# Late query blocks: P and q turned by VectorE before their trip through DRAM, and four slots of split queries

## The chip, the cores and the metric

The kernel runs on one core of a Trainium2 chip. The metric is the device time of one execution in microseconds (us), lower is better. Five engines work side by side, each through its own list of instructions in order: TensorE (PE in the profile; PEld is its loading of weights), VectorE (DVE), ScalarE (ACT), GpSimd (POOL) and SyncE (SP), which here does nothing but issue DMA transfers. An instruction that waits holds up everything behind it on its engine. SBUF is the on-chip memory of 128 partitions, PSUM holds what TensorE writes, and DRAM is the memory outside.

## What is computed

Attention with a gated memory, for 4 batches and 8 heads of 576 queries with 64 channels, and then a feed-forward layer on its 2304 x 512 output:

```python
scores = scale * np.matmul(q, k.transpose(0, 1, 3, 2))
scores = np.where(causal, -1000000000.0, scores)
a = np.exp(scores - scores.max(-1, keepdims=True))
a /= a.sum(-1, keepdims=True) + 1e-09
local = np.matmul(a, v)
q_p = phi(q)                                  # phi(x) = where(x > 0, x, exp(x) - 1) + 1
mem_out = (q_p @ M_prev) / ((q_p * z_prev).sum(-1) + 1e-06)
attn = g * mem_out + (1 - g) * local          # g = sigmoid(beta), one per head
h = np.maximum(np.maximum(x @ w1, x @ w2), x @ w3)   # x = attn as [tokens, 512]
out = h @ w_out
```

## The kernel before

**Tiling.** Queries are cut into an early half (rows 0 to 319) and a late half (rows 320 to 575). A pair is two heads of one batch in one half: 32 pairs, the 16 early ones first. Four pairs of one batch and half give one block of x, whose feed-forward work (the MoE pieces, on the PSUM tiles `bm`) is spread over the next four pairs. From pair 10 on (`FLIP`) and so in the whole late half, k and q come from DRAM already block-turned, in runs of 32 elements (128 B), and VectorE finishes the turning in 32 x 32 blocks.

**A late pair.** It has two units of 128 queries. For each head and unit:

- `scores` multiplies split queries (`qs`, a high and a low part in fp32r) with keys (`k1`) into the banks `bs`: 448 columns for the first unit, 2 x 288 for the second. VectorE masks and takes the least value (`masked`, into `p`), ScalarE takes the exponential, GpSimd normalises (`normal`). 64 columns of the memory term stand ahead of each unit in the same tile, so a first unit of P is 128 x 512 and a second one 128 x 640 for each head.
- P must be turned before `values` can multiply it with V (5 blocks of 128, two heads side by side, into `bv`). The second unit is turned by TensorE (`transpose_p`, into `bt`, copied to `pt` by ScalarE or VectorE).
- The first unit goes through DRAM. `swap_out` (line 779) writes it to `pd` with two DMAs in runs of 512 B and reads it back to `kq` with four DMAs of 32 partitions each in runs of 128 B. `swap_in` (line 794) turns the 32 x 32 blocks of `kq` on VectorE into `pt`, 128 x 512 for each head.
- q of a late pair is loaded by `load_qk` (line 547) with eight DMAs of 32 KB into the tile `rw`, each head twice (the low parts need the other half of the partitions), VectorE turns 128 x 256 for each head (`transpose_in`, line 804), and `split_q` (line 847) makes `qs` from it, with ScalarE or VectorE for the high part and VectorE or GpSimd for the low part. Three slots of `qs` serve all pairs, two are taken by each pair. A second copy of q (`rq`, not turned) is loaded for `phi`.

**What sets the order.** The functions only record operations in a `Plan`. `Plan.run` (line 333) is a list scheduler with a table of costs, estimated transfer times (`Plan.move`, line 223) and priorities; `SEEDS` (line 63) shakes the priorities a number of times. What it places is the order of each engine's list, SyncE's too, and the choice between two engines where an operation has two forms. Line 432 issues everything, so the engine and the names of the tiles tell the instructions apart, not the line. Up to the first MoE piece the scheduler puts dummy matmuls (line 396, on `bm` and `mask`) where it sees TensorE idle. Each DMA waits in SyncE's list for what it reads or overwrites.

Of the kernel before, what the change touches and what calls it, by code (L numbers as in the profile page):

```python
# [12 lines left out]
F32 = mybir.dt.float32  # L13
# [12 lines left out]
class Half:  # L26
# [33 lines left out]

NEAR = 2

SEEDS = (
    278295, 305439, 80682, 703233, 480040, 697831, 571163, 590513, 983183, 218641,
    429041, 460242, 338319, 945803, 848882, 158944, 676007, 966563, 564471,
)
# [11 lines left out]
class Plan:  # L78
# [31 lines left out]
    @staticmethod  # L110
    def region(ap):

        if ap.space == bass.MemoryType.DRAM:
            last = sum(st * (n - 1) for st, n in ap.ap)
            return 0, 1, ((ap.offset, ap.offset + last + 1),)
        dims = sorted(((abs(st), n) for st, n in ap.ap[1:] if n > 1 and st), reverse=True)
        row = ap.ap[0][0]
        p0, f0 = divmod(ap.offset, row)
        size = 1
# [6 lines left out]
        return p0, p0 + ap.ap[0][1], tuple((r, r + size) for r in runs)  # L126

# [38 lines left out]
    def cost(self, eng, name, kw):  # L166
# [6 lines left out]
        if eng == "pe":  # L173
            if name == "transpose":
                return 2.5 + 0.837 * kw["in_"].shape[0]
            if kw["rhs"].dtype != F32:
                return 13.3 + kw["rhs"].shape[-1] / 2.4
            if self.mode(name, kw)[0] == 64:
                return 106 + 1.67 * kw["rhs"].shape[-1] if out.shape[0] > 64 else 115
            return 1.69 * kw["rhs"].shape[-1]  # L180
        psum = any(
# [41 lines left out]
    def move(*aps):  # L223
# [6 lines left out]
        for ap in aps:  # L230
# [5 lines left out]
            piece = min(piece, run)  # L236
        return size / (180 if piece < 512 else 240)

# [94 lines left out]
    def run(self, prio, real):  # L333
# [124 lines left out]
def attention_memory_moe(ctx, tc, q, k, v, m_prev, z_prev, beta, w1, w2, w3, w_out, out):  # L458
# [42 lines left out]

    kq = tile_([128, 1280], F32, "rk")
    r_k = Ring.of(kq[:, 512 * i : 512 * i + 512] for i in range(2))
    r_kq = Ring.of(kq[:, 320 * i : 320 * i + 320] for i in range(4))
    r_q0 = Ring(cp, 2, [128, 3, 2, D], F32, "rq")
# [17 lines left out]
    r_in = Ring.of(kq_in[:, 320 * i : 320 * i + 320] for i in range(4))  # L523
    turned_in = kq_in[:, :1024]
    dp = ctx.enter_context(tc.tile_pool(name="dp", bufs=1, space=bass.MemoryType.DRAM))
    r_d = Ring(dp, 2, [8, 128, 128], F32, "pd")
    b_s = Ring(ps, 2, [128, 512], F32, "bs")
# [7 lines left out]
    P = Plan(nc)  # L535
    P.kept |= {t[:].tensor.name for t in r_d.tiles}

    r_w = Ring(cp, 3, [128, 1088], U32, "rw")
    r_g = Ring(cp, 2, [128, 512], F32, "g")
    r_pt = Ring(cp, 2, [128, 1152], F32, "pt")  # L540

# [6 lines left out]
    def load_qk(pi):  # L548
# [12 lines left out]
        else:  # L561
# [231 lines left out]

    def swap_in(pi):

        r = raw[pi]
        for e in range(2):
            r["pt", e] = r_pt.next()
            P.dve.transpose(
                out=r["pt", e][:, :1024].rearrange("p (t x) -> p t x", x=256)[:, :, :128],  # L800
                in_=turned_in[:, 512 * e : 512 * e + 512].rearrange("p (t x) -> p t x", x=128),
            )

    def transpose_in(pi, nm):
# [4 lines left out]
        if pi >= FLIP and nm == "k":  # L809
            for e in range(2):  # L810
                r["k1", e] = r_k1.next()
            for c0 in (0, 320)[: hi + 1]:
                c1 = c0 + HALVES[c0 > 0].n
                src = r_kq.next()[:, : c1 - c0]
                P.dve.transpose(out=src, in_=r["k"][:, c0:c1])
                split_k(pi, c0, c1, src)
            return
        if pi >= FLIP:
# [28 lines left out]
    def split_q(pi, e, src):  # L847

        r = raw[pi]
        n = HALVES[pairs[pi][1]].n  # L850
        r["qs", e] = r_q.next()
        qs = qs_all[:, r["qs", e] : r["qs", e] + 640].rearrange("p (a x) -> p a x", a=2)
        P.copy(("act", "dve"), out=qs[:, 0, :n], in_=src)
        P.combine(("dve", "pool"), ALU.subtract, out=qs[:, 1, :n], in0=src, in1=f(qs[:, 0, :n]))

# [9 lines left out]
    def product(pi, e, q0, rows, c0, c1, s, before=0, after=None):  # L865
# [8 lines left out]
        else:  # L874
            x0 = r["qs", e] + q0
            terms = [
                (qs_all[:, x - before : x + rows], r["k1", e][:, c0:c1]) for x in (x0, x0 + 320)
            ]
# [91 lines left out]
    def transpose_p(pi, e, u):  # L970
        b, hi, hp = pairs[pi]
        hf = HALVES[hi]
        r = raw[pi]
        j, q0, rows, ext = u
        if ("pt", e) not in r:
            r["pt", e] = r_pt.next()
        pt = r["pt", e]
        i = hf.units.index(u)
        p = r["pbuf", e][:, i * hf.pitch : i * hf.pitch + D + ext]
        step = 4 if j < 4 else 3  # L980
# [14 lines left out]
    def values(pi):  # L995
# [5 lines left out]
        for i in range(hf.kb):  # L1001
            c0 = next(u[1] for u in hf.units if u[0] >= i) if i else 0

            xs = [r["pt", e][:, hf.at(i) + c0 : hf.at(i) + n] for e in range(2)]
            for e in (1, 0):
                if not e:
                    P.tied.append(len(P.ops))
                P.pe.matmul(
                    after=xs[1 - e],
                    out=acc[64 * e : 64 * e + 64, c0:n],  # L1010
                    lhsT=r["v"][:, e, i - 1] if i else per_batch["mv", b][:, 2 * hp + e],
# [107 lines left out]
    for n in range(nheads + 2):  # L1119
        pieces = []  # L1120
        sc = pt = None
        if n < nheads:
            pi, e = heads[n]
            us = HALVES[pairs[pi][1]].units
            if pairs[pi][1]:
                sc = [(2 * us[e][3] * 0.425 + 100, partial(scores, pi, x, us[e])) for x in range(2)]
                if e == 0:
                    sc.append((0, partial(swap_out, pi)))
            elif pi >= FLIP:
# [32 lines left out]
        if n < nheads:  # L1162
# [79 lines left out]
```

## Time and profile before

| | us |
|---|---|
| median of 3 runs (lowest, highest) | 512.95 (511.92, 516.84) |
| the profiled execution | 520.21 |
| its span in the trace | 518.4 |
| TensorE busy | 497.5 |
| VectorE, ScalarE, GpSimd busy | 334.7, 296.6, 284.7 |

The profiled execution is 7.26 us longer than the median, so sums made on the trace are carried to the median with care. TensorE's busy time contains dummy matmuls and matmuls at the lower clock. The early pairs fill the first 225 us or so, the late pairs 225 to 478 us, and what is left is the feed-forward work of the last block.

### The profile page before, as it was taken

To read this page: it belongs to the slowest core of one execution; us is meant where nothing else is said; L and a number is where in the kernel's file an instruction comes from. 1 tells how busy PE (TensorE), PEld (TensorE's weight loads), DVE (VectorE), ACT (ScalarE), POOL (GpSimd) and SP (SyncE) were. 2 spreads that over 40 slices of the span, in tenths; PEclk is the share of its full clock that TensorE was granted. 3 is DMA by queue.
4 is the path that set the end of the run, shared out by engine and by line. 5 is a ranking of instruction groups with operands and counts; after the bars stand their busy time and mean duration, and the time that the engine had idled before them with its cause. 6 is when DMAs were issued, how large, how long until landed. Compare 5 with 4: busy or idle time off the path is not lost.

```text
span 518.4 us, 11066 instructions
## 1 busy us (share of the span) xinstructions
PE 497.5 (96%) x3507; PEld 433.2 (84%) x3507; DVE 334.7 (65%) x1137; ACT 296.6 (57%) x844; POOL 284.7 (55%) x444
## 2 busy tenths in 40 slices
PE   8998999999989999999888999799998999999997
PEld 6765788888988899989887789698887989997996
DVE  3699989976655685567456567677678787552120
ACT  4599888765554685466455456465656655543111
POOL 3578887687442583465455467556656667631000
PEclk9999999999989999999998999899999999999999
DMA  6866966645454553358765677878886736443001
GB/s 125 200 170 185 240 194 207 208 93 108 82 104 89 111 98 66 65 123 150 120 121 94 117 166 148 152 130 146 169 156 142 147 101 123 86 80 62 21 1 42
DMA packets 258522, 64.05 MB, mean 124 GB/s; under 512 B 227616, under 2 KB 255520, under 8 KB 258464
## 3 DMA queue, kind: packets, MB, share of 16 engines
q1 hardware_dynamic: 256832, 62.96, 58.3%
q8 instruction: 28, 0.46, 0.4%
q10 hardware_dynamic: 1632, 0.39, 0.3%
q14 instruction: 30, 0.25, 0.2%
HBM read 50.20 MB, written 13.11 MB: 122 GB/s over the span
## 4 chain that ended last, share of the span: by engine, by line
PE 67%; DVE 10%; DMA 9%; SPq 8%; issue 3%; ACT 2%; POOL 1%; ACTq 0%; DVEq 0%; POOLq 0%
PE bm L432 43%; PE bs L432 8%; SPq L432 8%; PE bv L432 7%; PE bt L432 7%; DMA kq<-pd 6%; DVE pt L432 3%; DVE p L432 2%; PE bm L396 2%; DMA rq<-in_q_dram 1%; DMA pd<-p 1%; POOL p L432 1%; DVE sum L432 1%; DVE k L432 1%; DVE bm L432 1%
## 5 line engine op out<-in xcount | busy, mean ns | idle before, releaser
L432 PE MATMUL bm<-xh,wh 128*128 128x320 f32 (+1 forms) x576 | 177.6, 309 | 0.6 <-ACT g L432 0.4
L432 PE MATMUL bm<-xl,wh 128*128 128x320 f32 (+1 forms) x576 | 172.5, 300 | 0.0
L432 PE MATMUL bm<-xh,wl 128*128 128x320 f32 (+1 forms) x576 | 172.0, 299 | 0.0
L432 POOL TENSOR_SCALAR p<-p,sum,gb 128x320 f32<-128x320 f32 (+3 forms) x128 | 86.8, 684 | 53.5 <-DVE sum L432 35.6
L432 PEld LDWEIGHTS bm<-xh,wh 128*128 128x128 f32 x576 | 110.7, 192 | 5.5 <-issue 2.7
L432 PEld LDWEIGHTS bm<-xl,wh 128*128 128x128 f32 x576 | 110.5, 192 | 1.0 <-issue 0.4
L432 PEld LDWEIGHTS bm<-xh,wl 128*128 128x128 f32 x576 | 110.3, 192 | 0.6 <-issue 0.4
L432 ACT ACTIVATE p<-p,st 128x192 f32<-128x192 f32 (+4 forms) x144 | 84.2, 586 | 35.2 <-DVE st L432 33.2
L432 DVE TENSOR_TENSOR t<-bm,t 128x320 f32<-128x320 f32 (+1 forms) x96 | 43.1, 449 | 68.6 <-PE bm L432 67.0
L432 DVE CUSTOM_DVE_ANT_0 p<-bs,mask 128x192 f32<-128x192 f32 (+3 forms) x128 | 59.5, 470 | 26.7 <-PE bs L432 26.4
L432 PE MATMUL bt<-ident,p 128*128 128x128 f32 x336 | 55.3, 278 | 9.4 <-ACT pt L432 5.7
L432 PE MATMUL bs<-k,qs 128*128 128x288 f32 (+5 forms) x264 | 56.8, 320 | 4.3 <-DVE st L432 4.3
L432 ACT COPY pt<-bt 128x256 f32<-128x256 f32 (+2 forms) x134 | 48.4, 388 | 19.9 <-PE bt L432 18.8
L432 PEld LDWEIGHTS bt<-ident,p 128*128 128x128 f32 x336 | 39.8, 140 | 19.2 <-POOL p L432 9.6
L432 POOL TENSOR_TENSOR p<-phf,nn 128x128 f32<-128x128 f32 (+1 forms) x96 | 36.9, 389 | 29.5 <-PE bt L432 15.6
L432 PEld LDWEIGHTS bs<-k,qs 128*128 128x128 f32 (+1 forms) x264 | 40.2, 190 | 7.4 <-DVE st L432 5.8
L432 POOL TENSOR_TENSOR qs<-rk,qs 128x256 fp32r<-128x256 f32 (+1 forms) x35 | 26.9, 770 | 31.6 <-ACT qs L432 25.5
L432 ACT CAST hh<-t 128x256 fp32r<-128x256 f32 x47 | 19.1, 406 | 43.0 <-DVE t L432 42.9
L432 PEld LDWEIGHTS bv<-pt,rv 128*64 128x64 f32 x384 | 28.4, 137 | 15.0
L432 PE MATMUL bv<-pt,rv 128*64 128x256 f32 (+1 forms) x384 | 40.7, 344 | 0.0
L432 DVE STREAM_TRANSPOSE rk<-rw 128x256 f32<-128x256 f32 (+1 forms) x82 | 36.8, 460 | 4.6 <-DMA rw<-in_k_dram 1.7
L432 PE MATMUL bm<-woh,hh 128*128 128x512 f32 (+1 forms) x102 | 39.4, 386 | 0.0
(93 smaller groups left out, 854.0 us busy)
## 6 DMA issues: line engine op xcount, KB each, us to landing
rw<-in_moe_w_dram SPq DMA_DIRECT2D x18, 512.0 KB, 4.1
pd<-p SPq DMA_DIRECT2D x32, 256.0 KB, 2.5
kq<-pd SPq DMA_DIRECT2D x64, 128.0 KB, 3.8
rq<-in_q_dram SPq DMA_DIRECT2D x74, 64.0 KB, 2.4
rw<-in_k_dram SPq DMA_DIRECT2D x64, 72.0 KB, 2.6
rw<-in_q_dram SPq DMA_DIRECT2D x128, 32.0 KB, 2.1
rv<-in_v_dram SPq DMA_DIRECT2D x32, 128.0 KB, 3.1
out_dram<-g SPq DMA_DIRECT2D x15, 256.0 KB, 2.1
```

The source lines that it names most:

```text
L396: self.nc.tensor.matmul(**filler)
L432: getattr(getattr(self.nc, self.ENGINES[e]), name)(**kw)
```

## The change

The P trip: VectorE turns the first unit of P in 32 x 32 blocks before the trip (`turn_p`, in place of `swap_out`), one DMA writes 128 rows of 4 KB to `dp`, and four DMAs read runs of 1 KB straight into `pt` (`move_p`, in place of `swap_in`). `pt` of the late half is one tile whose blocks lie 32 columns apart from each other's, so `values` reads the moving operand in runs of 32 elements, and ScalarE's copies into it write such runs. The second unit's five blocks are copied as 4 + 1 instead of 3 + 2.

The q trip: late pairs no longer load q turned. `turn_q` turns `rq` on VectorE (one 128 x 256 instruction for both heads), writes 128 rows of 1 KB to `dq`, and four DMAs read runs of 512 B into `rw`, from where `split_q` takes it with no further turning.

The split queries of late pairs have four slots of 512 columns instead of three of 640. Only pair 0 (before: pairs 0 and 1) loads its q through ScalarE's queue. The planner counts 110 bytes per ns for runs under 256 B (before: 180) and lets ScalarE begin at 700 ns; there are 26 other `SEEDS` (before: 19).

```diff
-NEAR = 2
+NEAR = 1
-        return size / (180 if piece < 512 else 240)
+        return size / (110 if piece < 256 else 180 if piece < 512 else 240)
-        free["sp"] = 700.0
+        free["sp"] = free["act"] = 700.0
...
-    qs_all = tile_([128, 64 + 3 * 640], F32R, "qs")
-    r_q = Ring.of(64 + 640 * i for i in range(3))
+    qs_all = tile_([128, 2048], F32R, "qs")
+    r_q = [Ring.of(64 + 640 * i for i in range(3)), Ring.of(512 * i for i in range(4))]
...
+    pt_late = pt_all[:, :2048].rearrange("p (a e i r) -> p e i a r", a=8, e=2, i=4)
...
-            for e in range(2):
+            if hi:
+                r["qt"] = t[:, kn : kn + 512]
+            for e in range(2 - 2 * hi):
                 r["qt", e] = t[:, kn + hf.n * e :][:, : hf.n]
...
-    def swap_out(pi):
+    def turn_p(pi):
         r = raw[pi]
-        r["pd"] = d = r_d.next()
         for e in range(2):
-            P.sp.dma_start(
-                out=d[4 * e : 4 * e + 4].rearrange("t q x -> q t x"),
-                in_=r["pbuf", e][:, :512].rearrange("q (t x) -> q t x", t=4),
+            P.dve.transpose(
+                out=turned_p.rearrange("p (c e i r) -> p e i c r", c=4, e=2, i=4)[:, e],
+                in_=r["pbuf", e][:, :512].rearrange("p (i c x) -> p i c x", i=4, c=4),
             )
+        r["pd"] = d = r_dp.next()
+        P.sp.dma_start(out=d, in_=turned_p)
+
+    def move_p(pi):
+        src = raw[pi]["pd"].rearrange("(a x) m -> x a m", x=32)
         for c in range(4):
             P.sp.dma_start(
-                out=turned_in[32 * c : 32 * c + 32].rearrange("r (k x) -> r k x", x=32),
-                in_=d[:].rearrange("k (a r) x -> r (k a) x", r=32)[:, :, 32 * c : 32 * c + 32],
+                out=pt_all[32 * c : 32 * c + 32, :1024].rearrange("p (a m) -> p a m", a=4),
+                in_=src[:, :, 256 * c : 256 * c + 256],
             )
-    def swap_in(pi):
-        r = raw[pi]
-        for e in range(2):
-            r["pt", e] = r_pt.next()
-            P.dve.transpose(
-                out=r["pt", e][:, :1024].rearrange("p (t x) -> p t x", x=256)[:, :, :128],
-                in_=turned_in[:, 512 * e : 512 * e + 512].rearrange("p (t x) -> p t x", x=128),
+    def turn_q(pi):
+        r = raw[pi]
+        t = r_qt.next()
+        P.dve.transpose(
+            out=t.rearrange("p (h b r) -> p b h r", h=2, b=4),
+            in_=r["q"].rearrange("p c e (h x) -> p (c e) h x", h=2),
+        )
+        d = r_dq.next()
+        P.sp.dma_start(out=d, in_=t)
+        src = d.rearrange("(a x) m -> x a m", x=32)
+        for g in range(4):
+            h = g % 2
+            P.sp.dma_start(
+                out=r["qt"][32 * g : 32 * g + 32].rearrange("p (a m) -> p a m", a=4),
+                in_=src[:, :, 128 * h : 128 * h + 128],
             )
...
+                xs = [pt_late[:, e, i] for e in range(2)]
...
-                sc.append((0, partial(swap_out, pi)))
+                sc.append((0, partial(turn_p, pi)))
...
+                if pairs[pi + 1][1]:
+                    tr.append((0, partial(turn_q, pi + 1)))
...
-            pieces.append((0, partial(swap_in, heads[n][0])))
+            pieces.append((0, partial(move_p, heads[n][0])))
```

**VectorE's list, at the first unit of a late pair.** The `ISA p,st` rows are the masks (448 columns for the first unit, 288 for the second), `k_3_85` is a split key, `t` an MoE tile. Before, this stands there:

```order
L432 ISA p,st<-bs_113,mask 128x448
L432 ISA st 128x1
L432 TENSOR_TENSOR k_3_85<-rk,k_3_85 64x256
L432 STREAM_TRANSPOSE pt_128<-kq 128x4x128
L432 STREAM_TRANSPOSE pt_129<-kq 128x4x128
L432 TENSOR_SCALAR sum<-sum 128x1 x2
L432 STREAM_TRANSPOSE rk<-rw_124 128x320
L432 RECIPROCAL sum<-sum 128x1 x2
L432 ISA p,st<-bs_114,mask 128x448
```

Behind the masks of a later late pair the change has:

```order
L436 TENSOR_SCALAR sum<-sum 128x1
L436 TENSOR_TENSOR t_104<-bm_120,t_104 128x256
L436 RECIPROCAL sum<-sum 128x1
L436 STREAM_TRANSPOSE kq<-p 128x4x4x32 x2
L436 TENSOR_TENSOR t_104<-bm_121,t_104 128x256
L436 ISA p,st<-bs_115,mask 128x288
L436 ISA st 128x1
```

A few rows ahead of these, the change turns q of the next pair (`rq` to `rk`), between the two 288-column masks that precede the pair's first-unit masks:

```order
L436 ISA p,st<-bs_115,mask 128x288
L436 ISA st 128x1
L436 STREAM_TRANSPOSE rk<-rq_90 128x4x2x32
L436 ISA p,st<-bs_116,mask,st 128x288
L436 ISA st 128x1
L436 TENSOR_TENSOR k_1_83<-rk,k_1_83 64x320
L436 ISA p,st<-bs_115,mask 128x448
```

Before, the two turnings of P read `kq`, which a DMA fills, and stand between the two masks of the next pair; now they read `p`, which GpSimd writes, and stand behind both masks of their own pair.

**SyncE's list over about one late pair.** `rw` from `in_q` is q, `rw` from `in_k` is k, `rv` is v, `rq` is q for phi. Before:

```order
L432 DMA rw_124<-in_q_dram 32x8x32
L432 DMA kq<-pd_112 32x32x32 x4
L432 DMA rv_96<-in_v_dram 128x4x64 x2
L432 DMA rw_124<-in_q_dram 32x8x32 x7
L432 DMA z_93<-in_z_prev_dram 128x256
L432 DMA rw_125<-in_q_dram 32x8x32 x4
L432 DMA pd_111<-p 128x4x128
L432 DMA rw_125<-in_k_dram 32x18x32 x2
L432 DMA pd_111<-p 128x4x128
L432 DMA rq_90<-in_q_dram 128x2x64 x2
L432 DMA rw_125<-in_k_dram 32x18x32 x2
```

And in the change:

```order
L436 DMA dp_111<-kq 128x1024
L436 DMA rw_125<-dq_114 32x4x128 x4
L436 DMA rq_90<-in_q_dram 128x2x64 x2
L436 DMA rv_97<-in_v_dram 128x4x64 x2
L436 DMA pt<-dp_111 32x4x256 x4
L436 DMA dq_113<-rk 128x256
L436 DMA rw_125<-in_k_dram 32x18x32
L436 DMA rw_126<-dq_113 32x4x128 x4
L436 DMA dp_112<-kq 128x1024
L436 DMA rq_91<-in_q_dram 128x2x64 x2
```

The eight short loads of q are gone, two writes of P have become one, and one write and four reads of q have come in; both reads stand a few rows behind the write whose landing they wait for.

**ScalarE's list between two pairs' scores.** Before, where the second-unit copies to `pt` end and the next pair's keys are split:

```order
L432 COPY pt_129<-bt_116 128x256
L432 ACTIVATE phf_88<-rq_91 128x256
L432 CAST hh<-t_104 128x256
L432 CAST k_2_84<-rk 64x320
L432 ACTIVATE p,sum<-p,st 128x576
```

And in the change:

```order
L436 COPY pt<-bt_118 128x128
L436 ACTIVATE phf_88<-rq_91 128x256
L436 CAST qs<-rw_126 128x256
L436 CAST hh<-t_104 128x256
L436 CAST k_2_84<-rk 64x320
L436 CAST k_2_84<-rk 64x256
L436 ACTIVATE p,sum<-p,st 128x576
```

The cast that makes split queries now reads `rw`, which the q trip fills, and not `rk`, which VectorE fills.

## Rows read from the trace of the kernel before

**Rows 1.** Page, part 4, and the chain of waits of 225 to 478 us by line

```profile
PE 67%; DVE 10%; DMA 9%; SPq 8%; issue 3%; ACT 2%; POOL 1%; ACTq 0%; DVEq 0%; POOLq 0%
by line: PE bm L432 31.3%; DMA kq<-pd 12.9%; SPq L432 12.4%; PE bv L432 8.9%; PE bs L432 7.2%; DVE pt L432 4.5%; PE bt L432 4.0%; issue 3.8%; DVE p L432 2.8%; DMA pd<-p 2.2%; POOL p L432 1.6%; DVE k L432 1.5%; DVE sum L432 1.1%; DVE rk L432
```

**Rows 2.** Waits of PE, 225 to 478 us: total us, times, longest

```profile
PE bs L432 <- DVE st L432: 4.3, 4, 2.1
PE bt L432 <- POOL p L432: 3.2, 2, 3.0
PE bt L432 <- ACT pt L432: 3.0, 1, 3.0
PE bv L432 <- issue: 0.9, 1, 0.9
```

**Rows 3.** Windows: length, busy PE PEld DVE ACT POOL, PEclk, DMA share, GB/s

```profile
100.00:225.00 125.00, 122.31 (x816) 110.67 (x815) 81.17 (x292) 74.21 (x231) 67.08 (x113) 0.99 0.48 92
225.00:350.00 125.00, 116.60 (x804) 104.21 (x804) 78.09 (x270) 67.98 (x186) 71.68 (x105) 0.97 0.73 136
350.00:478.00 128.00, 124.74 (x931) 110.25 (x928) 84.24 (x287) 70.74 (x194) 73.34 (x103) 1.00 0.64 123
420.00:475.00 55.00, 54.63 (x416) 48.49 (x415) 32.62 (x112) 28.27 (x78) 28.89 (x42) 1.00 0.51 96
```

**Rows 4.** Timeline, PE at three stalls: start, us, work, [idle before <-releaser]

```profile
260.63 0.74 PE L432 MATMUL bt<-ident,p 128*128 128x128 f32 x5 [3.03 <-ACT pt L432]
...
330.36 0.77 PE L432 MATMUL bt<-ident,p 128*128 128x128 f32 x5 [2.96 <-POOL p L432]
...
390.59 0.54 PE L432 MATMUL bs<-k,qs 128*128 128x288 f32 x2 [1.36 <-DVE st L432]
```

**Rows 5.** Timeline, VectorE shortly ahead of those three stalls

```profile
256.79 1.30 DVE L432 STREAM_TRANSPOSE pt<-kq 128x512 f32<-128x512 f32 x2 [4.22 <-DMA kq<-pd]
...
327.37 1.30 DVE L432 STREAM_TRANSPOSE pt<-kq 128x512 f32<-128x512 f32 x2 [3.50 <-DMA kq<-pd]
...
388.60 1.30 DVE L432 STREAM_TRANSPOSE pt<-kq 128x512 f32<-128x512 f32 x2 [2.25 <-DMA kq<-pd]
```

**Rows 6.** Waits of VectorE, 225 to 478 us: total us, times, longest

```profile
DVE pt L432 <- DMA kq<-pd: 25.0, 12, 4.2
```

**Rows 7.** Timeline, SyncE's list around one pair's reading of P

```profile
284.44 2.92 SPq L432 DMA_DIRECT2D rw<-in_q_dram  x6
287.41 2.59 SPq L432 DMA_DIRECT2D kq<-pd  x4
```

**Rows 8.** DMA issues of 300 to 360 us: count, KB each, median us to landing

```profile
pd<-p SPq DMA_DIRECT2D x8, 256.0 KB, 2.4
kq<-pd SPq DMA_DIRECT2D x16, 128.0 KB, 3.8
rw<-in_q_dram SPq DMA_DIRECT2D x36, 32.0 KB, 2.5
rw<-in_k_dram SPq DMA_DIRECT2D x14, 72.0 KB, 2.6
```

**Rows 9.** Landing of all reads of P, from the view of the tile kq

```profile
DMA to landing us min/median/max: 2.6/3.8/5.5
```

**Rows 10.** Groups by shape on VectorE: busy us, mean ns, idle before

```profile
L432 DVE STREAM_TRANSPOSE pt<-kq 128x512 f32<-128x512 f32 x32 | 20.9, 690 | 25.0 <-DMA kq<-pd 25.0
L432 DVE STREAM_TRANSPOSE rk<-rw 128x256 f32<-128x256 f32 x48 | 20.3, 432 | 1.3 <-POOL qs L432 0.9
```

**Rows 11.** Chain of waits in order of time: start, us, what

```profile
12.38 3.00 PE bm L396 x27
...
423.79 2.10 PE bv L432 x20
...
425.89 0.73 PE bs L432 x4
...
430.85 1.43 PE bm L432 x12
...
473.68 0.76 PE bt L432 x5
```

More of the change, by code (lines that the diff above doesn't have):

```diff
@@ L58 @@
 FILL_GAP, FILL_WARM, FILL_FROM, WARM = 60, 80, 450, 7500
[L61 removed]
+NEAR = 1
 SEEDS = (
[L64 to L65 removed]
+    170495, 618851, 839998, 870954, 887498, 687841, 346258, 191154, 388799, 372867,
+    129018, 780087, 981015, 378067, 878635, 152620, 533197, 991412, 299355, 70786,
+    899701, 937121, 576273, 847781, 388742, 446033,
 )
@@ L115, in region @@
             return 0, 1, ((ap.offset, ap.offset + last + 1),)
-        dims = sorted(((abs(st), n) for st, n in ap.ap[1:] if n > 1 and st), reverse=True)
         row = ap.ap[0][0]
+        dims = sorted(
+            ((abs(st), n) for st, n in ap.ap[1:] if n > 1 and st and st % row), reverse=True
+        )
         p0, f0 = divmod(ap.offset, row)
+        p1 = p0 + ap.ap[0][1] + sum(st // row * (n - 1) for st, n in ap.ap[1:] if st % row == 0)
         size = 1
@@ L125, in region @@
             runs = [r + i * st for r in runs for i in range(n)]
-        return p0, p0 + ap.ap[0][1], tuple((r, r + size) for r in runs)
+        return p0, p1, tuple((r, r + size) for r in runs)
     @staticmethod
@@ L176, in cost @@
             if kw["rhs"].dtype != F32:
-                return 13.3 + kw["rhs"].shape[-1] / 2.4
+                return 13.3 + n / 2.4
             if self.mode(name, kw)[0] == 64:
-                return 106 + 1.67 * kw["rhs"].shape[-1] if out.shape[0] > 64 else 115
-            return 1.69 * kw["rhs"].shape[-1]
+                return 106 + 1.67 * n if out.shape[0] > 64 else 115
+            return 1.69 * n
         psum = any(
@@ L813, in transpose_in @@
                 c1 = c0 + HALVES[c0 > 0].n
-                src = r_kq.next()[:, : c1 - c0]
+                src = kq[:, c0:c1] if hi else r_kq.next()
                 P.dve.transpose(out=src, in_=r["k"][:, c0:c1])
                 split_k(pi, c0, c1, src)
+            return
+        if hi:
+            for e in range(2):
+                split_q(pi, e, r["qt"].rearrange("p (a c e r) -> p e c a r", a=4, c=2, e=2)[:, e])
             return
@@ L849, in split_q @@
         r = raw[pi]
[L850 to L854, printed above, removed]
+        hi = pairs[pi][1]
+        n = HALVES[hi].n
+        r["qs", e] = o = r_q[hi].next()
+        hl = [qs_all[:, x : x + n] for x in (o, o + n)]
+        if hi:
+            hl = [x.rearrange("p (c a r) -> p c a r", c=2, a=4) for x in hl]
+        P.copy(("act", "dve"), out=hl[0], in_=src)
+        P.combine(("dve", "pool"), ALU.subtract, out=hl[1], in0=src, in1=f(hl[0]))
     def split_k(pi, c0, c1, src):
@@ L876, in product @@
             terms = [
-                (qs_all[:, x - before : x + rows], r["k1", e][:, c0:c1]) for x in (x0, x0 + 320)
+                (qs_all[:, x - before : x + rows], r["k1", e][:, c0:c1]) for x in (x0, x0 + HALVES[pairs[pi][1]].n)
             ]
@@ L974, in transpose_p @@
         j, q0, rows, ext = u
+        i = hf.units.index(u)
+        p = r["pbuf", e][:, i * hf.pitch : i * hf.pitch + D + ext]
+        if hi:
+            t = b_t.next()
+            for i in range(4):
+                P.pe.transpose(
+                    out=t[:, 128 * i : 128 * i + 128], in_=p[:, 128 * i : 128 * i + 128], identity=ident
+                )
+            P.copy(
+                ("act", "dve"),
+                out=pt_late[:, e, :, 4:],
+                in_=t.rearrange("p (i a r) -> p i a r", i=4, a=4),
+            )
+            t = b_t.next()[:, :128]
+            P.pe.transpose(out=t, in_=p[:, 512:640], identity=ident)
+            P.copy(("act", "dve"), out=pt_all[:, 2048 + 128 * e : 2176 + 128 * e], in_=t)
+            return
         if ("pt", e) not in r:
@@ L1002, in values @@
             c0 = next(u[1] for u in hf.units if u[0] >= i) if i else 0
-            xs = [r["pt", e][:, hf.at(i) + c0 : hf.at(i) + n] for e in range(2)]
+            if not hi:
+                xs = [r["pt", e][:, hf.at(i) + c0 : hf.at(i) + n] for e in range(2)]
+            elif i < 4:
+                xs = [pt_late[:, e, i] for e in range(2)]
+            else:
+                xs = [pt_all[:, 2048 + 128 * e : 2176 + 128 * e] for e in range(2)]
             for e in (1, 0):
```

21 lines of the change are left out of this document (12 added, 9 removed).

## The prediction

> **What bounds the kernel now.** I read the page first: the chain that ended last is TensorE for two thirds of the span, and next to it stand DMA and SyncE's list with 9% and 8% [rows 1]. So TensorE is the bound, and time can only be had where it waits. In the stretch of the late pairs the same chain looks otherwise: the reading back of P (`kq<-pd`) holds 12.9% of it and SyncE's own issuing 12.4% [rows 1]. TensorE's waits there add up to 4.3 + 3.2 + 3.0 + 0.9 = 11.4 us in 8 waits [rows 2], and the windows say the same: 253 us less 116.60 and 124.74 busy leave 11.7 [rows 3]. The granted clock is 0.97 in the first of these windows and 1.00 in the second [rows 3]. A mean of 0.97 over 125 us is time at 1.2 GHz instead of 2.4; it has cost 0.03 x 125 = 3.7 us of work. Loss in the late pairs: 11.4 + 3.7 = 15.1 us of the profiled 520.21.
>
> Who causes the waits? TensorE names three different engines [rows 2], so I looked at what VectorE did just before the longer ones. Each time it had stood still for the reading of P: TensorE idle 3.03, 2.96 and 1.36 us [rows 4], VectorE idle before turning `kq` 4.22, 3.50 and 2.25 us [rows 5]. The reader is to see one cause under three names: VectorE's list is in order, the turning waits for the DMA, and the masks behind it hold up ScalarE, GpSimd and in the end TensorE. All in all VectorE waited 25.0 us in 12 such waits [rows 6]. The differences 1.19, 0.54 and 0.89 us, 0.9 in the mean, are what the other engines absorb: a wait of an engine off the bound costs about its length less 0.9 us.
>
> Why the reading is late is in SyncE's list: six loads of q, 2.92 us, directly ahead of the four readings, which take 2.59 to issue [rows 7], and these land 3.8 us after issue in the median, 5.5 at worst [rows 9].
>
> **The change, part by part.**
>
> *P trip.* On VectorE nothing is saved in count: two 128 x 512 turnings of 0.690 us [rows 10] a pair, before and after. What changes is what they wait for: GpSimd's result and not a DMA. That takes all 25.0 us of VectorE's waits on `kq<-pd` away, and with them the stalls of [rows 4]. The new place has a cover: the turned rows go to DRAM, come back and are read by TensorE in `values`, which stands about a pair later; nothing else waits for them. The length of this trip, from the last turning on: the write lands in 2.4 us by the pd row of half its size, or 3.8 as an upper bound; then four issues (2.59) and 3.8 to land [rows 7, 8], 8.8 to 10.2 us together. A late pair takes about 14 us, and the turnings stand behind the first unit's masks, so `values` finds them landed, with some 4 us to spare. The reads now overwrite `pt` and must wait for the preceding `values` (2.10 us [rows 11]); that ends before the write has landed, so I cost it at nothing. If that cover were gone, SyncE would stand still, and loads of k and v behind it would come late.
>
> *Packets.* By sizes and run lengths, a late pair moves P and q in 1024 + 4096 + 2048 = 7168 packets before, and in 128 + 512 + 128 + 512 = 1280 after; k's 2304 of 128 B stay. DMA was busy 0.73 and 0.64 in these windows [rows 3]. I cost this at no time of its own: it only makes landings shorter, between nothing and the 1.2 us by which the median 3.8 stands over the minimum 2.6 [rows 9]. The Trainium skill (DMA: Bandwidth & Descriptors, Specifications) asks for at least 512 B for full rate, which P's reads and q's now reach; the trace agrees in kind, as 128 KB in 128 B runs took 3.8 us and 256 KB in 512 B runs 2.4 [rows 8].
>
> *SyncE.* A pair issued 2 + 4 for P and 8 for q; now 1 + 4 and 1 + 4. Four issues of 0.49 us (2.92 / 6 [rows 7]) are saved, 2 us a pair. Against it stands one more wait for a landing, dq's, with at most one or a few rows of cover in the list: up to 2.4 us [rows 8]. I count the two as even.
>
> *q trip.* VectorE does one 128 x 256 turning instead of two, 0.432 us less a pair [rows 10], off the bound. But q now arrives over two landings, and ScalarE's cast waits for the second. From the order: the turning stands between the 288-column masks; the cast stands behind the copies of the second five transposes. Between lie 36 matmuls at 1.43 us for 12, ten transposes at 0.76 for five, and the four 448-column score matmuls, 0.73 x 448 / 288 = 1.1 us [rows 11]: 6.9 us, less about 0.9 for mask and turning, 6.0 us. The trip takes 2.4 for the write, three further issues of 0.49, and 2.5 to 3.8 for the last read [rows 7, 8], 6.4 to 7.7 us. So ScalarE waits 0.4 to 1.7 us a pair. With 0.9 us absorbed, the lower end costs nothing and the upper 0.8 us a pair, 12.8 us over 16 pairs. I take the lower half, because DMA has fewer packets in flight, and cost it at nothing, and keep the rest for a rival.
>
> The Trainium skill (DMA: Bandwidth & Descriptors, Anatomy of one DMA) speaks against such trips: some 2 us of each transfer are completion, most of all for writes to DRAM, whatever their size. The shortest median here, 2.4 us [rows 8], agrees; by the rule the q trip would be 4.0 us plus issues and bytes, which changes no term above.
>
> *Four slots.* The second head's cast need no longer wait for the preceding pair's scores. It was one cause of slack, not of a stall among [rows 2]; a gain of 0.
>
> *Strided operand of values.* TensorE reads four of five blocks in runs of 32 elements. No row before shows such an operand. Below: nothing. Above: a matmul of 256 columns takes 1.43 / 12 = 0.119 us [rows 11], 0.012 more than 256 columns at 2.4 GHz; if each further run cost as much, 7 x 0.012 for each of eight pairs of strided matmuls are 0.7 us a pair of heads, 11 us in all, an estimate from that row. I take 0, since within a run it reads as before. The Trainium skill (SBUF — State Buffer, Door 1: The DMA port swizzle, its note on cachelines) would have only the 16-byte step matter, and a run here is eight of them; no run shows it yet.
>
> *Start.* By the order, 135 dummies stand before the first `values` instead of 116. At 3.00 us for 27 [rows 11] that is 0 to 2.1 us; I take 1.0.
>
> *What stays.* A new plan has stalls of its own. The quietest stretch, 420 to 475, lost 0.4 us in 55; the stretch ahead of the late pairs, without P trips, 2.7 idle and 0.01 x 125 = 1.3 by the clock in 125 [rows 3]. Over 253 us that is 1.7 to 8.1 us; middle 4.9.
>
> **The sum.** 15.1 - 4.9 - 1.0 = 9.2 us off the profiled 520.21, that is 511.0. The median is 7.26 lower. If that excess has nothing to do with these stalls, the median becomes 512.95 - 9.2 = 503.7. If all of it is these stalls, the median has only 7.8 of 15.1 to lose: (15.1 - 4.9) x 7.8 / 15.1 - 1.0 = 4.3, or 508.7. I take the middle, **506.2**.
>
> **Rivals.**
> 1. *Same: the waits only change their engine.* ScalarE (q cast) waits at the middle of its range and somewhat over, 1.3 us: 0.4 x 16 = 6.4 us back, and the median comes to 506.2 + 6.4 = 512.6. For it: the trip has no slack by the sum above. Against it: 25.0 us of VectorE's waits are gone, and ScalarE is less busy than VectorE [rows 3].
> 2. *Slower: the q trip bounds the pair.* If the last read lands 5.5 us after issue, as the worst of kq did [rows 9], the trip is 9.4 us, ScalarE waits 3.4, TensorE 2.5 a pair: 40 us, and even half of the pairs give 506.2 + 20 = 526. It decides from a wait of about 1.9 us a pair on: (1.9 - 0.9) x 16 = 16 us against the 9.2 gained. Against it: those 5.5 us were among 7168 more small packets.
> 3. *Strided operand.* At its bound of 11 us: 517, still no change. Nothing in the rows speaks for it.
> 4. *All stalls go*: 512.95 - 15.1 + 1.0 = 498.9. The quiet stretch [rows 3] speaks for it, the start and the chance that the median had fewer stalls against it.
>
> **How the numbers follow.** Forecast with its own spread (500 to 510) 0.62, all stalls gone 0.06, rivals 1 and 3 0.20, rival 2 0.12. About 1% is what a measurement here can tell from no change: 507.8 and 518.1. Of the forecast's 0.62, 0.52 lie below 507.8. Faster 0.52 + 0.06 = 0.58; same 0.10 + 0.20 = 0.30; slower 0.12. The range reaches from 499 to 515, which leaves out rival 2, the far end of rival 3 and a little below; the likeliest case's own range is 500 to 510.
>
> **What would show it.** Right: no wait of VectorE on a DMA of P, the turnings behind GpSimd; VectorE's 25.0 us gone; TensorE's waits in the late pairs under 6 us; DMA share well under 0.7 there; granted clock 1.00 in all late windows. Wrong: ScalarE or GpSimd waiting on `rw<-dq` for more than 1 us in most pairs; TensorE waiting on `pt<-dp` at `values`; `values` longer than 2.10 us for 20 matmuls; SyncE standing still ahead of `pt<-dp` with k late behind it; the first `values` more than 2 us later.

## The result, and the profile after

| | before | after |
|---|---|---|
| median (lowest, highest), us | 514.89 (511.92, 517.37), 4 runs | 500.74 (500.31, 501.68), 4 runs |
| profiled execution, us | 520.21 | 501.68 |
| its span, us | 518.4 | 499.6 |

The ratio of after to before is 0.973, with a 95% interval of 0.9665 to 0.9795: faster by 2.7%. (A fourth run of before, 517.37, moved its median from 512.95.) One execution of `before_newplan` below took 514.12 us at a mean granted clock of 0.977, where its other five had 0.993 to 0.997, and is left out of its figures.

The chain that ended last, by engine and by line, of the whole of after:

```profile
PE 88%; ACT 3%; DVE 3%; DMA 2%; SPq 2%; issue 1%; POOL 0%; ACTq 0%; DVEq 0%
PE bm L436 57%; PE bv L436 11%; PE bs L436 10%; PE bt L436 9%; SPq L436 2%; DMA rq<-in_q_dram 1%; PE bm L400 1%; DMA rw<-in_moe_w_dram 1%; DVE k L436 1%; ACT p L436 1%; DVE p L436 1%; ACT pt L436 0%; ACT kq L436 0%; POOL p L436 0%; ACT phe L436 0%
```

TensorE holds 88% of it where it held 67% [rows 1]; no transfer of P is in it any more. All waits of TensorE in the late pairs (which now end at about 465 us), as total, times, longest:

```profile
PE bt L436 <- POOL p L436: 0.6, 2, 0.3
```

Before, these were 11.4 us [rows 2]. The windows of the late pairs (length, busy PE, PEld, DVE, ACT, POOL, granted clock, DMA share, GB/s) have TensorE busy for all but 0.7 of 240 us, at a clock of 1.00 in both, where it was 0.97 in the first [rows 3]:

```profile
225.00:350.00 125.00, 124.68 (x875) 111.28 (x875) 91.91 (x305) 73.52 (x203) 71.09 (x102) 1.00 0.62 159
350.00:465.00 115.00, 114.58 (x877) 102.25 (x874) 74.21 (x252) 62.92 (x171) 57.07 (x82) 1.00 0.45 126
```

Of VectorE's waits in the same stretch, these two rows answer to the 25.0 us of [rows 6]. The turnings wait a little for GpSimd, as the code says, and the turning of q for its load:

```profile
DVE kq L436 <- POOL p L436: 4.2, 11, 0.7
...
DVE rk L436 <- DMA rq<-in_q_dram: 1.7, 2, 1.3
```

The new transfers (count, KB each, median us from issue to landing):

```profile
dp<-kq SPq DMA_DIRECT2D x16, 512.0 KB, 3.1
pt<-dp SPq DMA_DIRECT2D x64, 128.0 KB, 3.1
...
rw<-dq SPq DMA_DIRECT2D x64, 64.0 KB, 2.1
```

**Where the time went.** From the first `values` of the last early pair to that of the last late pair before took 475.53 - 229.81 = 245.7 us and after 456.69 - 226.15 = 230.5. These 15.2 us are the 15.1 that the prediction had called the loss of the late pairs, all of it. Another 3.7 (229.81 - 226.15) lie in the early pairs, nearly all of them behind the start: the fourth pair's `values` begins at 46.32 us in before and at 46.05 in after. From there to the last early pair before took 183.5 us and after 180.1; runs with before's very lists for the early pairs took 180.5 to 183.1 (`q_merged`, `swap_deferred`, `kq_long` below), so up to 3 us of it is how before's profiled execution fell out.

### The profile page after: what moved, and what is told of

Read it like the earlier page. It is cut to its first block, busy times and chain, and to the rows that moved or that the text cites. A ratio compares the mean times of both kernels' runs of the same rounds, so it can differ in the third digit from the quotient of the medians.

```text
span 499.6 us, 10997 instructions
## 1 busy us (share of the span) xinstructions
PE 489.8 (98%) x3528; PEld 426.9 (85%) x3528; DVE 342.3 (69%) x1152; ACT 292.6 (59%) x832; POOL 274.0 (55%) x425
## 4 chain that ended last, share of the span: by engine, by line
PE 88%; ACT 3%; DVE 3%; DMA 2%; SPq 2%; issue 1%; POOL 0%; ACTq 0%; DVEq 0%
PE bm L436 57%; PE bv L436 11%; PE bs L436 10%; PE bt L436 9%; SPq L436 2%; DMA rq<-in_q_dram 1%; PE bm L400 1%; DMA rw<-in_moe_w_dram 1%; DVE k L436 1%; ACT p L436 1%; DVE p L436 1%; ACT pt L436 0%; ACT kq L436 0%; POOL p L436 0%; ACT phe L436 0%
## 5 line engine op out<-in xcount | busy, mean ns | idle before, releaser
L436 PEld LDWEIGHTS bm<-xh,wh 128*128 128x128 f32 x576 | 109.5, 190 | 5.1 <-issue 1.9
L436 PEld LDWEIGHTS bm<-xh,wl 128*128 128x128 f32 x576 | 108.9, 189 | 0.3
L436 ACT ACTIVATE p<-p,st 128x320 f32<-128x320 f32 (+4 forms) x144 | 84.1, 585 | 22.5 <-DVE st L436 20.3
L436 ACT COPY pt<-bt 128x256 f32<-128x256 f32 (+4 forms) x135 | 49.6, 388 | 29.3 <-PE bt L436 28.4
L436 PE MATMUL bt<-ident,p 128*128 128x128 f32 x336 | 56.7, 280 | 4.2 <-ACT pt L436 3.4
L436 PE MATMUL bs<-k,qs 128*128 128x288 f32 (+5 forms) x264 | 54.9, 312 | 0.0
L436 PE MATMUL bv<-pt,rv 128*64 128x256 f32 (+1 forms) x384 | 42.4, 345 | 0.0
L436 PE MATMUL bm<-woh,hl 128*128 128x512 f32 (+1 forms) x102 | 39.0, 383 | 0.3 <-DVE hl L436 0.3
L436 PE MATMUL bm<-wol,hh 128*128 128x512 f32 (+1 forms) x102 | 38.6, 381 | 0.0
```

The costliest lines, as they stand in the source:

```text
L436: getattr(getattr(self.nc, self.ENGINES[e]), name)(**kw)
```

## Experiments

Three theories went into them. A: VectorE's wait, and what stands behind it in its list. B: P simply comes back late, because of short packets and SyncE's list. C: the planner's new constants and seeds. The runs were made in three groups, each beside its own runs of before: 512.81 us for the first (`p_alone`, `q_alone`, `after_oldplan`, `wait_back`), 514.24 for the second (those of 3 and 4) and 514.68 for the third (those of 6 and `before_newplan`). Gains are against the group's own before.

**1. Each trip alone.** `p_alone` is the change without its q trip, its four slots and its planner's numbers:

```diff
-    r_q = [Ring.of(64 + 640 * i for i in range(3)), Ring.of(512 * i for i in range(4))]
+    r_q = Ring.of(64 + 640 * i for i in range(3))
...
-                if pairs[pi + 1][1]:
-                    tr.append((0, partial(turn_q, pi + 1)))
```

> The P trip alone: VectorE turns P first, runs of 4 KB out and 1 KB in, straight into the operand of values; q, the three slots, the planner's constants and the seeds are those of before. Theory A (VectorE standing still for the reading of P is what stalls TensorE): about 502 us, -12, and no wait of VectorE on a DMA of P. Theory B (late landings: short packets and SyncE's long list; q's eight short loads are still there): 506 to 510. Theory C (the new seeds and constants bring the gain): 514, give or take 5, since its seeds were not found for it.

Measured: 498.93 us (497.26 to 500.09), ratio 0.9716 (0.9669 to 0.9764). TensorE has no wait at all left in its late pairs, and VectorE none for a DMA. The P trip alone does all that the change does, and more than any of the theories had expected of it.

`q_alone` is the other half: q trip and four slots, with `swap_out` and `swap_in` as before and the old planner's numbers.

> The q trip and the four slots alone, P as before, planner and seeds of before. Theory A: 511 to 515, and VectorE still waits some 20 us on the reading of P. Theory B: 504 to 508, since SyncE has four issues and 2048 packets less a pair and P's reads come earlier. Theory C: 514 give or take 5.

Measured: 503.39 us (502.82 to 504.83), ratio 0.981 (0.9764 to 0.9856). It leaves P's trip as it was, and yet two thirds of the gain are there. VectorE's waits for transfers in the late pairs:

```profile
DVE rk L435 <- DMA rq<-in_q_dram: 9.8, 7, 3.2
DVE pt L435 <- DMA kq<-pd: 8.0, 10, 2.6
```

The wait for P fell from 25.0 to 8.0 us although P's readings landed no sooner (median 3.9 us): VectorE comes to the turning 3.2 us behind their last issue in the median, where it came after 2.2 in before. 13.9 and 9.4 us don't add up to the 12 to 14 of both: the two halves remove the same stalls.

**2. The planner's numbers, taken back and put in alone.** `after_oldplan` is the change with before's `NEAR`, rate, start and seeds.

> The changed kernel with the seeds, the constants and the start of before. Theories A and B: 501 to 504, a microsecond or two over the changed kernel for want of fitting seeds. Theory C: 510 or more.

Measured: 499.47 us (498.73 to 501.96), ratio 0.9746 (0.9689 to 0.9802). The change needs none of them, and I put theory C aside. That was too quick. The opposite run, `before_newplan`, is the kernel before with those numbers only:

```diff
-        return size / (180 if piece < 512 else 240)
+        return size / (110 if piece < 256 else 180 if piece < 512 else 240)
```

> The kernel before with the change's planner alone: 110 bytes per ns for short runs, ScalarE from 700 ns on, one pair's first loads instead of two through ScalarE, and the 26 new seeds; every operation and transfer as before. Theory C (the new plan is the gain): 500 to 504 us. Theory B (P comes back late): short runs are now counted as slower by the planner, so it may leave the reading back more room; I expect half of the stalls at most to go, 507 to 513 us, and VectorE to wait 12 us or more for the reading back of P.

Measured: 506.12 us (505.41 to 507.36), ratio 0.9845 (0.9816 to 0.9874): 8.6 us, with every operation and transfer of before. VectorE, for which I had expected 12 us or more, waits for P no more at all; the one wait for a transfer in its late pairs is

```profile
DVE rk L433 <- DMA out_dram<-g: 1.6, 1, 1.6
```

P lands as late as ever (min/median/max, from the view of the tile `kq`), and the DMA share from 225 to 350 us is higher than before, not lower, while TensorE doesn't stand still there for a moment (its 3.7 us of waits in the late pairs come behind 350 us):

```profile
DMA to landing us min/median/max: 2.7/3.8/5.1
```

```profile
225.00:350.00 125.00, 125.00 (x880) 112.09 (x879) 84.29 (x294) 75.88 (x208) 81.64 (x116) 1.00 0.79 150
```

What differs is where the turning stands. One pair, SyncE's list and then VectorE's:

```profile
297.16 2.46 SPq L433 DMA_DIRECT2D kq<-pd  x4
```

```profile
305.33 1.30 DVE L433 STREAM_TRANSPOSE pt<-kq 128x512 f32<-128x512 f32 x2
```

From the end of the last issue (299.62) to the turning are 5.7 us, and there is no wait in brackets. In before the issues of [rows 7] end at 290.00, and the turning that reads them is this one:

```profile
293.60 1.30 DVE L432 STREAM_TRANSPOSE pt<-kq 128x512 f32<-128x512 f32 x2 [3.95 <-DMA kq<-pd]
```

VectorE was there at 289.65, before the last issue had ended. Over all 16 late pairs VectorE comes to the turning 0.7 us before to 4.1 us after the last issue in the kernel before (median 2.2), and 5.1 to 9.9 us after it here (median 6.4). The 3.8 us of a landing are counted from each issue's own start; from the end of the last issue, P has landed after 2.7 to 3.9 us in before (median 3.4) and after 3.0 to 4.6 here (median 3.3). By the planner's old rate four readings of 131072 B take 4 x 131072 / 180 = 2.9 us, by the new one 4.8. I did not part the rate from the 26 seeds, `NEAR` and ScalarE's start.

**3. Only the place of VectorE's turnings.** `swap_deferred` is before with these two instructions let go ten rows later in VectorE's list (or ahead of the first that needs them), all other lists untouched:

```diff
+            op.hold = 10
...
+                if op.hold:
+                    held.append(op)
```

> The kernel before, with one edit: VectorE's two turnings of P (kq to pt) stand ten instructions later in its list; every other list, all transfers and the plan are those of before. Theory A (masks queued behind the wait are what stalls TensorE): VectorE's 25 us of waits on P's reading shrink to a few us and the time falls by 6 to 12 us, to 501 to 507. Theory B (it is the transfers' own lateness that has to go; the data come too late in any case): values is then held up itself, 511 to 515.

Measured: 511.46 us (507.5 to 512.94), ratio 0.9923 (0.9894 to 0.9952), 2.8 us. VectorE's wait is gone (1.5 us of 25.0 are left; it now comes 2.2 to 9.1 us after the last issue), but TensorE waits in a new place (total, times, longest):

```profile
PE bv L440 <- DVE pt L436: 4.6, 3, 2.4
PE bv L440 <- ACT p L440: 1.5, 1, 1.5
PE bv L440 <- ACT k L440: 1.5, 1, 1.5
PE bv L440 <- ACT phe L440: 1.3, 1, 1.3
PE bv L440 <- DVE sum L440: 0.9, 1, 0.9
```

9.8 us at `bv`, the `values`, and 11.3 with the other waits, in place of 11.4 elsewhere: `values` now begins 0.2 us (median) behind the end of the turnings, and P has landed 2.0 us (median) before they begin. A later turning without a later or better placed `values` moves the stall to the reader of `pt`. Theory A, by which it is enough to take VectorE's wait away, does not hold in this form; other distances than ten rows were not tried.

**4. Only the transfers.** Three runs change what is issued, and leave every list as planned. `kq_long` reads P back in runs of 1 KB (512 packets a pair instead of 4096):

```diff
+            op.real = dict(
+                out=turned_in[32 * c : 32 * c + 32].rearrange("p (a m) -> p a m", a=4),
+                in_=rows[:, :, 256 * c : 256 * c + 256],
+            )
```

> The kernel before with P's four reads in runs of 1 KB instead of 128 B (4096 packets a pair become 512), the same bytes, the same lists; P comes back in another arrangement, which changes values and no work. If packets are what makes P's reads late: the reads land in about 3 us instead of 3.8, 503 to 508. If SyncE's list is: 510 to 514, since each read is issued as late as before.

Measured: 502.58 us (501.31 to 504.42), ratio 0.9761 (0.9718 to 0.9803): 11.7 us by run length alone. The landing's median went from 3.8 to 3.3 us, and a read takes less time to issue, too (ns, min/median/max, in before and in `kq_long`):

```profile
L432 SPq DMA_DIRECT2D kq<-pd x64: 320/562/2397, 232.9 to 467.1; - x64
...
L434 SPq DMA_DIRECT2D kq<-pd x64: 320/430/1678, 230.1 to 450.2; - x64
```

From the first issue to the last landing P takes 5.0 us (median) instead of 6.2. VectorE's wait went from 25.0 us to

```profile
DVE pt L434 <- DMA kq<-pd: 10.7, 7, 3.9
```

`q_merged` loads late q in four DMAs of 64 partitions instead of eight, so that SyncE has four issues fewer a pair ahead of P's readings, with the same packets:

```diff
+                        op.real = "none" if i % 2 else dict(
+                            out=to[32 * i : 32 * i + 64].rearrange("p (c d) -> p c d", d=32),
```

> The kernel before with late q loaded in four DMAs of 64 partitions instead of eight of 32, the same bytes in the same runs of 128 B, the plan's lists otherwise untouched; rows of q land on other partitions than they should, which changes values and no work. It takes four issues of about 0.5 us a pair from SyncE's list and leaves every packet. If SyncE's list is what makes P's reads late: 502 to 507 and VectorE's waits under 10 us. If packets are: 511 to 515.

Measured: 509.53 us (505.23 to 511.38), ratio 0.9892 (0.9834 to 0.995), 4.7 us, between what the two theories had expected; P's landing is unchanged (3.9), and VectorE's wait is

```profile
DVE pt L434 <- DMA kq<-pd: 17.2, 13, 4.2
```

So SyncE's list was a cause too, by these medians the smaller one.

`p_short` goes the other way: the full change, with P read in runs of 128 B again.

> The changed kernel with P's four reads in runs of 128 B instead of 1 KB, as before the change, the same bytes, the same lists; P comes back in another arrangement, which changes values and no work. If packets carry the gain: 505 to 510. If who waits carries it (nothing but values waits for these reads now, a few us later): 500 to 502, with landings near 3.8 us.

Measured: 501.46 us (499.68 to 502.44), ratio 0.9743 (0.9704 to 0.9783), no slower than the change by anything that could be told. The transfer itself is slower again:

```profile
pt<-dp SPq DMA_DIRECT2D x64, 128.0 KB, 3.8
```

It took 3.1 in the change, and TensorE's waits in the late pairs are the same 0.6 us. The same 4096 packets a pair that cost 11.7 us in before cost nothing here, with q's short loads gone as well; P turned first, in short runs and with before's loads of q, was not run.

**5. VectorE's wait put back.** `wait_back` is the change with one small copy on VectorE that waits for P's four readings, as `swap_in` did:

```diff
+        P.dve.tensor_copy(out=mask_top[:, :1], in_=pt_all[:, :1])
```

> The changed kernel with one tiny VectorE copy a late pair (one column of pt) that waits for the landing of P's four reads, recorded where swap_in was. Theory A: VectorE waits again, 16 waits of up to 2 us, and the time rises by 3 to 10 us over the changed kernel. Theory B: the landings are early now, the copy finds them done, under 1 us more. Theory C: nothing.

Measured: 500.68 us (499.45 to 501.72), ratio 0.9752 (0.9706 to 0.9798). The copy hardly waited:

```profile
DVE mask_top L436 <- DMA pt<-dp: 1.8, 2, 1.6
```

So this run could not price the wait: the planner put the copy behind the landing in most pairs. It shows that a VectorE instruction that needs this transfer costs nothing that can be measured where it comes after the landing.

**6. The slots, and the change beside the P trip on one chip.** `three_slots` takes the fourth slot away:

```diff
-    r_q = [Ring.of(64 + 640 * i for i in range(3)), Ring.of(512 * i for i in range(4))]
+    r_q = [Ring.of(64 + 640 * i for i in range(3)), Ring.of(512 * i for i in range(3))]
```

> The full change with three slots of split queries in the late half instead of four. My step said that the fourth slot is worth 0: within 1 us of the full change. If the slot is what gives the query trip its time, ScalarE's cast waits for the preceding pair's scores and the time is 505 or more. The planner's lists move a little too, since the slot is one of the things that it waits for; a difference of 1 to 2 us would be put down to that.

Measured: 500.97 us (499.32 to 502.88), ratio 0.9741 (0.9711 to 0.977). The fourth slot is worth nothing that can be measured.

`changed_again` and `p_again` are the change and `p_alone` once more, in the same group.

> The full change once more, on the same chip as the next three, so that differences under one per cent between them can be read. All theories: 500 to 501.5 us, ratio 0.97 to 0.98 to the kernel before.

> The P trip alone (old q loads, three slots, the planner's old constants and seeds), beside the full change on one chip. If late landings of P were all that cost (theory B), nothing is left for the q trip and the slots to remove once the P trip is there: within 1.5 us of the full change, on either side. If the q trip and the slots have a gain of their own, this kernel is 2 us or more slower than the full change; if the q trip costs something by itself (a second landing for each pair), it is 1.5 us or more faster.

Measured: 501.44 us (499.42 to 503.82), ratio 0.9747 (0.9712 to 0.9781), and 499.03 (497.61 to 501.28), ratio 0.9709 (0.9678 to 0.974). The P trip alone is ahead by 2.4 us here, as it was, with 498.93, in the first group; the intervals overlap, so I claim only that the q trip and the slots add nothing to it. Nor are the 2.4 us the price of the q trip, since `p_again` has before's planner too. The pair that differs in the q trip and the slots alone is `after_oldplan` and `p_alone`, in one group: 499.47 and 498.93 us, 0.5 apart, with ranges that overlap. The P trip with before's planner is the fastest kernel of the study.

**All of them on one scale.** For each profiled execution, the length of the stretch from the first `values` of the last early pair to that of the last late pair, TensorE's waits in the late pairs, and the difference (us):

| | stretch | TensorE's waits | difference |
|---|---|---|---|
| before | 245.7 | 11.4 | 234.3 |
| `swap_deferred` | 241.9 | 11.3 | 230.6 |
| `q_merged` | 235.6 | 4.9 | 230.7 |
| `before_newplan` | 234.6 | 3.7 | 230.9 |
| `q_alone` | 233.9 | 2.9 | 231.0 |
| `kq_long` | 233.1 | 3.3 | 229.8 |
| after | 230.5 | 0.6 | 229.9 |
| `p_alone` | 229.4 | 0 | 229.4 |

In before, 3.7 us of the clock come on top [rows 3], which leaves 230.6; in the other seven the granted clock is 1.00 in this stretch. So the late pairs take 229 to 231 us of TensorE's work in every one, and the runs differ in the waits that they leave and in whether the clock falls. That is also why 14.3 us less of VectorE's waits are worth so much in `kq_long`: 8.1 us of TensorE's waits and the 3.7 us of the clock are gone with them. The 0.9 us that the prediction has the other engines absorb in each wait fits roughly: 10.7 - 7 x 0.9 = 4.4 us for `kq_long` (measured 3.3), 17.2 - 13 x 0.9 = 5.5 for `q_merged` (4.9), 25.0 - 12 x 0.9 = 14.2 for before (11.4); for `q_alone`, 8.0 us in 10 waits, it would leave nothing (2.9).

## Why the prediction was right, and where its sum was off

The direction, the range and the core of the mechanism held; the forecast of 506.2 was 5.5 us too high, and the measured 500.74 lies next to rival 4 (498.9), which I had given 0.06. Point by point:

- **One cause under three names: right.** All of VectorE's 25.0 us are gone, and the 15.1 us of the late pairs with them (15.2 between the two `values` above). But the place of the turnings is not the only cure. `swap_deferred` takes VectorE's waits away and keeps TensorE's, and the longer runs of the P trip, which I had priced at nothing, bring 11.7 us without it (`kq_long`). What all the stalls have in common is P coming back too late for the first instruction that needs it; each trip moves that, and so does the new plan alone, and how the gain divides among them cannot be read from these runs.
- **What stays, 4.9 us: the step that failed.** TensorE waits 0.6 us in the late pairs, at a clock of 1.00. I had taken the new plan's stalls from other stretches of before (1.7 to 8.1 us). The runs show what I should have looked at: the room. In before, the turning stood in the middle of P's way, 2.2 us (median) behind the end of the last issue, for a landing 3.4 behind it, while `values` stood 5.0 to 13.8 us behind it (median 8.5). The change takes the turning out of that stretch; what then waits for the landing is `values` alone, and its distance from the last issue is still 5.0 to 13.0 (median 8.6), for a landing 2.8 behind it. The distances in before could be read beforehand, and gave no reason for a remainder. My "some 4 us to spare" for this place was about right (1.9 us at least, 5.8 in the median), and I didn't let it bear on the sum.
- **Start, a loss of 1.0 us: about right in size, in the wrong place.** Where the start ran undisturbed (last section), `values` of the fourth pair begins at 44.8, 44.1 and 44.7 us with the new planner's start (`wait_back`, `p_short`, `three_slots`) and at 43.4, 43.4, 42.9, 43.7, 43.8 and 43.5 with the old one (`p_alone`, `q_alone`, `after_oldplan`, `swap_deferred`, `q_merged`, `kq_long`): 1 us later. But the first `values`, which 19 more dummies were to delay, begins no later, at 19.8 us in those three and at 19.8 to 20.8 in those six. Between the two TensorE waits no longer (1.4 to 2.2 us against 1.6 to 3.0), so what costs the 1 us stays open. And 3.00 us for 27 dummies [rows 11] was not their usual price (last section). The new plan wins the loss back in the early pairs behind the start: `values` of the last early pair begins at 224.2 us (mean of those three) against 225.0 (mean of those six), 0.8 us earlier, which I had not looked for.
- **From the profile to the median: wrong.** I let half of the stalls be a peculiarity of the slow profiled execution. The median lost 14.2 us (12.2 from the first three runs), so the stalls were in the usual runs in full. The profiled execution was long for other reasons, at least in part: its fourth `values` begins 2.5 to 3.4 us later than in the six just named. With 15.1 less 0.6, and 0.8 for the early pairs, the whole 15.3 us taken from 512.95 give 497.7, and from 514.89 give 499.6; measured are 500.74.
- **Packets, at no time of their own: right for the changed kernel, wrong for before.** `p_short` shows nothing for 4096 packets a pair and `kq_long` 11.7 us. The 1.2 us by which P is back sooner decide only where an instruction in order stands at the landing's edge. The rule of the Trainium skill (DMA: Bandwidth & Descriptors, Specifications) that runs should be of 512 B or more agrees in kind: 128 KB landed in 3.8 us in runs of 128 B and in 3.1 in runs of 1 KB, in the same list.
- **SyncE, even: not wholly.** Four issues fewer were worth 4.7 us in before (`q_merged`). In the change SyncE stands still 9.6 us in 4 waits for `dq`'s landing, and TensorE's late waits name no transfer.
- **q trip, 0 of 0.4 to 1.7 us a pair: right.** ScalarE has no wait for `rw<-dq` among those of 225 to 465 us; its casts wait for a free slot, that is for TensorE (total, times, longest):

```profile
ACT qs L436 <- PE bs L436: 19.2, 8, 3.4
```

  So the cast is held by the scores ahead, not by the second landing, and rivals 1 and 2 did not come. The trip's landings are 1.7 to 4.3 us (median 2.2). The Trainium skill's rule on some 2 us of fixed cost, most of it completion (DMA: Bandwidth & Descriptors, Anatomy of one DMA), was measured there on transfers that GpSimd issues, which the prediction does not say. These here, which SyncE issues, agree with it, but it speaks against nothing where the time is covered.
- **Four slots, 0: right** (`three_slots`). But the slack that I had seen in them did not come either: before, the same wait of ScalarE's casts was

```profile
ACT qs L432 <- PE bs L432: 18.3, 12, 3.1
```

- **Strided operand, 0 of up to 11 us: right.** `values` of the late pairs (busy us, mean ns, idle before; the matmuls of 256 columns from 232 us on) in after, with most blocks strided:

```profile
L436 PE MATMUL bv<-pt,rv 128*64 128x256 f32 x192 | 23.4, 379 | 0.0
```

  and in before, with none:

```profile
L432 PE MATMUL bv<-pt,rv 128*64 128x256 f32 x192 | 23.5, 379 | 0.0
```

  They take the same time. Rival 3 falls.
- **The turnings keep their price:** 709 ns each instead of 690, with 4-dimensional patterns on both sides, 32 x 0.019 = 0.6 us in all, off the bound.

What stays open: how much of `before_newplan`'s 8.6 us is the rate of 110 and how much the seeds; how the gain of the P trip divides between the place of the turnings and the longer runs; and what the new start loses between the first and the fourth `values`.

## What to carry to other kernels

Where an engine's list is in order, compare for each transfer its landing with the distance from its issue to the first instruction that needs it, and take the work that depends on it out of that stretch: here the turnings cost nothing before the trip, and behind it they stood at the landing's edge and held up three engines. Causes that feed one edge (run length, issues ahead in a queue, a planner's rate) each recover a third to four fifths of the gain alone (4.7 to 11.7 of 14 us), so measure them one by one before you add their gains. When a stall's cause is gone and the next deadline has room by the same rows, forecast the whole stall as gone.

## What the runs showed that I had not expected

**The same start can take two lengths.** `p_alone` and `p_again` are one kernel. In the one, the start reads (start, us, work):

```profile
7.99 0.80 PE L435 MATMUL bs<-kq 64*128 64x320 f32 x2
...
9.67 1.68 PE L399 MATMUL bm<-mask 128*128 128x128 bf16 x27
```

and in the other:

```profile
9.34 1.43 PE L435 MATMUL bs<-kq 64*128 64x320 f32 x2
...
12.36 3.06 PE L399 MATMUL bm<-mask 128*128 128x128 bf16 x27
```

Between 10 and 20 us the granted clock reads 1.00 for both, which would be the higher of its two levels, 2.4 GHz, and yet the second takes nearly twice as long for the same matmuls. From start to start a dummy takes 0.107 us there and 0.056 in the first. 0.107 us is the pace at which the dummies begin in every execution, and again in after near 27 us, where the granted clock has fallen to the lower level, 1.2 GHz; so the second start ran at the pace of the lower level without the granted clock showing it. The quicker pace comes after 16 us in it and in before, and by 11 us in the other twelve. By the fourth pair's `values` the two executions of this kernel are 43.39 and 46.06 us in: 2.7 us. Before's profiled execution had the long start too, the other six with the old planner's start had the short one. With the new start none shows this, but in three of six executions (after among them) the clock falls in 20 to 30 us, behind a wait of TensorE for ScalarE that ends near 24 us: it was 2.2 to 2.3 us in those three (2.21 in after) and 0.7 to 1.5 in the others. That window of after, and then of `three_slots`, where it stayed at the higher level:

```profile
20.00:30.00 10.00, 7.79 (x59) 5.27 (x55) 6.44 (x25) 5.47 (x17) 4.14 (x9) 0.83 0.80 220
```

```profile
20.00:30.00 10.00, 8.56 (x74) 5.38 (x72) 8.07 (x32) 6.83 (x22) 5.00 (x11) 1.00 0.85 224
```

A price read from the first 20 us of one execution, as my 3.00 us for 27 dummies, may be twice the usual one; nothing here shows why the quicker pace comes late.

**A new plan of the same work brings more than half of the gain.** The same operations, with runs under 256 B counted at 110 instead of 180 B per ns, other seeds and a slightly different start, gained 8.6 of the 14 us, at a DMA share of 0.79 where it had been 0.73.
